# A retention layer and a squared-ReLU network on one core: filler matmuls from the first microseconds, another order of the loads, and a last output in three parts

## The chip, the core and the metric

The kernel runs on one core of one Trainium2 chip. The core has a matrix engine (PE, whose weight loads are listed as PEld), three engines for element-wise work (DVE, ACT, POOL), a queue engine (SP) that issues transfers, and 16 DMA engines that carry them between the main memory and the on-chip memory. Matrix products land in PSUM, of which the kernel holds four banks `fps` and two larger tiles, `sc` and `yy`. The metric is the device time of one execution in microseconds (us).

## The reference

Inputs are `q`, `k`, `v` of 4 x 8 x 768 x 64 floats (batch, head, time, width) and two weights of 512 x 2048 and 2048 x 512. The first half is a linear recurrence with a decay per head:

```python
for t in range(S):
    state = gamma[None, :, None, None] * state + np.einsum('bhd,bhe->bhde', k[:, :, t], v[:, :, t])
    y[:, :, t] = scale * np.einsum('bhd,bhde->bhe', q[:, :, t], state)
```

The second half takes the result with the heads side by side as `x` (3072 tokens x 512) and computes `h = max(x @ w_in, 0)` and `(h * h) @ w_out` in 32-bit floats.

## The kernel before, in words

**Tiling.** Time is cut into chunks of 128 tokens: 6 chunks for each of 4 batches, 24 in all (`m` or `n` below, 0 to 23). Within a chunk the recurrence becomes matrix products: scores of `k` against `q`, masked; values; and a state of 64 x 64 per head that is carried from chunk to chunk. Factors of the decay are multiplied in where `v` is cast (L434, L599) and where the result is read out (L573, L760). Matrices are cast from 32-bit to 16-bit floats on DVE, ACT or POOL (one helper, `copy_on`, L399 to L403), since PE works on 16-bit operands here.

The first four chunks go in pairs (0 with 1, 2 with 3): one load of 512 KB for each of `q`, `k`, `v` of a pair, transposes on PE (`T...`, L447), scores (`A`, L478), sums for the state (`B`, L494), values and the state's share (`C`, L504 and L515), read-out (`Y`). Later chunks have loads of 256 KB each (L588). Chunks 4 to 6 are transposed on PE through PSUM (L641), chunk 7 on PE as part of a visit (L614), and chunks 8 to 23 by a transposing DMA that SP issues (`X8` to `X23`, L632). A "visit" `V9.10` (L684, L695, L658, L673) finishes chunk 9 and does the scores of chunk 10; those need X10.

**The network.** Chunks are gathered in blocks (`BLOCKS`). `F1` (L807) is one group of the first product, 512 columns of PSUM: 8 matmuls of 256 columns in the first blocks, 4 of 512 or 16 of 128 in others. ACT applies the ReLU while it reads PSUM (L812), and DVE squares (L817). `F2.m.j` (L851) is a quarter of the second product of chunk `m`, 4 matmuls of 512 columns; its quarter `j` needs the weight slice `w_out j`. ACT copies the sum to an output tile `osb` (L859) and SP stores it (L863).

**Weights.** `w_in` comes in six pieces, four of 512 KB (`i0` to `i3`: the halves of its first two slices) and two of 1 MB (`i4`, `i5`); `w_out` in four of 1 MB (`o0` to `o3`). Each is cast in pieces (`cw...`) before use (L781 loads).

**Order.** All operations are put into a list with their dependencies, and `Plan.schedule` (L68) places them before the program is built, with assumed durations and an assumed model of the transfers. What comes out is a fixed order of instructions on each engine; each engine then runs its own in that order and waits for the data. `ORDER` (L228) fixes the order of the first loads on SP, all later transfers follow the plan, and `HOME` (L226) pins some casts to an engine. The same planner decides where "fillers" go: matmuls of the identity that nobody reads. The trace of before has two of them (L905), at 16.3 us.

```python
if WARM - WARMING < t < WARM + 1:
    o["fill"] = int(max(0.0, t - max(eng_free[eng], WARM - WARMING) - 0.1) / FILL)
```

Here `t` is the planned start of a PE operation, `WARM` is 20.0, `FILL` 0.215 and `WARMING` 5.5, so fillers stand between 14.5 and 21 us of the plan; they write to the last of four PSUM banks, which is kept free until then. The last chunk's output (`F2.23`) is made in two halves of 256 columns.

Of the kernel before, what the change touches and what calls it, by code (L numbers as in the profile page):

```python
# [14 lines left out]
AF = mybir.ActivationFunctionType  # L15
# [3 lines left out]
class Plan:  # L19
# [48 lines left out]
    def schedule(self, nbanks, max_open):  # L68
# [17 lines left out]
                    pool[e].add(o["i"])  # L86
        if "PE" in eng_free:
            eng_free["PE"] = 0.06 * PRE
        bank_free = [0.0] * (nbanks - 1) + [WARM + 1]
        bank_of = {}  # L90
        open_groups = set()
        closed = {}
# [5 lines left out]
        while done < n:  # L98
# [25 lines left out]
            if move:  # L124
# [4 lines left out]
                while sum(x[1] for x in out_) + n_desc > self.RING:  # L129
                    t = max(t, out_.pop(0)[0])  # L130
            start[i] = t
            b = o["bank"]
            if b is not None and b[0] == "open":
                k = min((x, j) for j, x in enumerate(bank_free) if x is not None)[1]
# [4 lines left out]
            if move:  # L139
                eng_free[eng] = t + hold  # L140
                if n_desc:
                    made = max(made, t + self.GEN_LATENCY) + gen
                    ready = made + 0.15
                else:
                    ready = t + hold + 0.5
                pipe = max(max(pipe, t + self.DMA_LATENCY) + cost, ready)
                late = [y for y in (max(max(y, t + self.DMA_LATENCY) + cost, ready) for y in late) if y > pipe + 0.05]
                end[i] = max([pipe] + late) + self.LAND
                out_.append((max([pipe] + late), n_desc))
                dur = hold  # L150
            else:
                if eng == "PE":
                    o["fill"] = 0
                    if WARM - WARMING < t < WARM + 1:
                        o["fill"] = int(max(0.0, t - max(eng_free[eng], WARM - WARMING) - 0.1) / FILL)
                    issued += 2 * o["fill"]
                    before = issued
                    todo, per = 2 * o["count"], dur / max(1, 2 * o["count"])
                    now = t
                    while issued + todo > edge:  # L160
                        step = max(0, edge - issued)
                        now = max(now + step * per, next_fetched)
                        issued, todo = max(issued, edge), todo - step
                        ahead = next((y for x, y in reversed(history) if x <= edge - self.AHEAD), 0.0)
                        ahead = max(ahead, crossed)
                        crossed = now
                        edge += self.BLOCK
                        next_fetched = ahead + min(5.7, max(0.3, pipe - ahead)) + self.FETCH
                    issued += todo
                    dur = now + todo * per - t  # L170
                    history.append((issued, t + dur))
                    if any(before < x <= issued for x in range(self.BLOCK0 - self.AHEAD, issued + 1, self.BLOCK)):
                        late.append(max(pipe, t + 0.4) + 1.27)
                    o["dur"] = dur
                eng_free[eng] = t + dur
                end[i] = t + dur + o["lat"]
# [26 lines left out]
AHEAD = 4  # L203
WARM = 20.0
FILL = 0.215
WARMING = 5.5
PACE = 8
LEAD = 2
NPE = 7
# [1 line left out]
PRE = 0  # L211
WHALF = 2
WHALFD = (0.60, 1.47, 33, 0.6)
CVT = {'DVE': 0.69, 'POOL': 1.1}
TCAST = {'DVE': 0.43, 'ACT': 0.63, 'POOL': 0.78}
TEVAC = {'ACT': 0.6, 'DVE': 0.62}
NPAIR = 2
F2LAG = 3.0
F2WAIT = 4
CAST = {"k": {"DVE": 0.43, "ACT": 0.63, "POOL": 0.78}, "q": {"DVE": 0.43, "ACT": 0.63, "POOL": 0.78}}  # L220
WCAST = {"DVE": 0.43, "ACT": 0.63, "POOL": 0.78}
EVAC = {"ACT": 0.6, "DVE": 0.62}
WPRIO = {"in": -2.0, "out": 2.0}


HOME = {'ck5': 'ACT', 'cq5': 'ACT', 'Eq0.0': 'DVE', 'cv0.0': 'DVE', 'ck0.0': 'DVE', 'cwin5.2': 'DVE', 'cv2.1': 'POOL', 'ck2.0': 'DVE', 'cwin5.0': 'DVE', 'cwin2.0': 'POOL', 'cwout0.3': 'POOL', 'cwin1.0': 'POOL', 'ck0.1': 'DVE', 'ck2.1': 'DVE'}  # L226
RANK = {}
ORDER = (  # L228
    "q0 k0 o0 i0 v0 q2 k2 o1 v2 i1 v4 i2 k4 i3 i4 q4 i5 k5 v5 v6 o2 o3 q5 v7 k6 q6 k7 q7"
)  # L230


# [8 lines left out]
def kernel(  # L241
# [279 lines left out]
    def pair_visits(m):  # L521
# [3 lines left out]
        for b2 in range(2):  # L525
            pl.add(f"A{m}.{b2}", "PE", 0.4, [f"qkT{q0}.{x}.{b2}" for x in "kq"] + [f"qkT{q0 + c}.{x}" for c in range(2) for x in "kq"],
                   banks[b2], lambda b2=b2: pair_scores(m, b2), prio=-300 + m, lat=0.25, count=16)
            for a in range(2):
                pl.add(f"P{m}.{b2}{a}", "DVE", 0.68, (banks[b2][a], "cmask2"), (f"ptp{w}.{b2}{a}",),
                       lambda b2=b2, a=a: nc.vector.tensor_tensor(  # L530
                           out=pts2[w][:, b2, a], in0=held_by[b2][:, a, :].rearrange("s (g j t) -> s g j t", g=2, j=2),
                           in1=cmask2[:, :, None, :].to_broadcast([P, 2, 2, C]), op=ALU.mult),
                       prio=urgency(m))
        tw = [f"twin{x}{w}.{b2}" for x in "kv" for b2 in range(2)]
        for c in range(2):
            if c == 1 and i + 1 == NCH - 1:
                continue
            o1 = {}
            i0 = pl.add(f"B{m + c}", "PE", 0.3, tw, (f"gB{m + c}",),
                        lambda c=c, o1=o1: pair_sums(m, c, fps[o1["op"]["bank_index"]]), prio=-290 + m, lat=0.25,  # L540
                        count=16, bank=("open", ("B", m + c), False))
            o1["op"] = pl.ops[i0]
            twin_users.append(i0)
            j0, j1 = state(m + c, 0), state(m + c + 1, 0)
            first = i + c == 0

            def add_up(j0=j0, j1=j1, first=first, o1=o1):
                cc = fps[o1["op"]["bank_index"]][:, 0:256].rearrange("s (p t) -> s p t", p=NJ)
                if first:
                    nc.vector.tensor_copy(sts[j1][:], cc)  # L550
                else:
                    nc.vector.tensor_tensor(out=sts[j1][:], in0=cc, in1=sts[j0][:], op=ALU.add)
            pl.add(f"S{m + c}", "DVE", 0.42, (f"gB{m + c}",) if first else (f"gB{m + c}", f"S{j0}"), (f"S{j1}",), add_up,
                   prio=urgency(m) - 0.5, bank=("close", ("B", m + c)))
        for b2 in range(2):
            def values_and_state(b2=b2):
# [272 lines left out]
    def rows(m):  # L829
        return where(m)[0] * S + where(m)[1] * C  # L830

    def ffn2(blk):
        for q4 in range(blk0[blk], blk0[blk] + blocks[blk]):
            g, u = divmod(q4, 4)
            h2 = h2s[g % NH2]
            slot = q4 % NOSB
            parts = 2 if q4 == NM - 1 else 1
            w = DM // parts
            for part in range(parts):
                ns = slice(part * w, part * w + w)  # L840
                grp = ("f2", q4, part)
                keys = [f"osb{slot}.{part}"] if parts > 1 else [f"osb{slot}.0", f"osb{slot}.1"]
                o1 = {}
                for j in range(4):
                    reads = [f"h{g % NH2}.{u}.{4 * j + c}" for c in range(4)] + [f"wout{j}.{c}.{h}" for c in range(4) for h in range(2)]

                    def mm(j=j, o1=o1, h2=h2, u=u, ns=ns, w=w):
                        ps = fps[o1["op"]["bank_index"]]
                        for c in range(4):
                            fb = 4 * j + c  # L850
                            nc.tensor.matmul(ps[:, 0:w], lhsT=h2[:, fb, u * C : u * C + C], rhs=w_out_bf[j][:, c, ns],  # L851
                                             start=(fb == 0), stop=(fb == NFB - 1))
                    i0 = pl.add(f"F2.{q4}.{j}" + f"/{part}" * (parts > 1), "PE", 0.866 / parts, reads, (f"g{grp}",), mm,
                                prio=(q4 + F2LAG) * 8 + 2 * j + 1 + part * 9, lat=0.2,
                                bank=("open", grp, True) if j == 0 else ("use", grp), count=4)
                    if j == 0:
                        o1["op"] = pl.ops[i0]
                pl.add(f"O{q4}" + f"/{part}" * (parts > 1), "ACT", 0.2 + 0.4 / parts, (f"g{grp}",), keys,
                       lambda o1=o1, slot=slot, ns=ns, w=w: nc.scalar.activation(  # L859
                           osbs[slot][:, ns], fps[o1["op"]["bank_index"]][:, 0:w], AF.Copy),  # L860
                       prio=q4, bank=("close", grp))
                pl.add(f"st{q4}" + f"/{part}" * (parts > 1), "SP", STORE, keys, (),
                       lambda q4=q4, slot=slot, ns=ns: nc.sync.dma_start(out[rows(q4) : rows(q4) + C, ns], osbs[slot][:, ns]),  # L863
                       prio=-1)

    dma_prio = {x: n for n, x in enumerate(dma_order(NM))}
# [30 lines left out]
    if tc is not None:  # L897
        with tc.manual_schedule():
# [3 lines left out]
            for i in sequence:  # L902
                o = pl.ops[i]
                for _ in range(o.get("fill", 0)):
                    nc.tensor.matmul(fps[NBANK - 1][:, 0 : 2 * P], lhsT=ident[:],  # L905
                                     rhs=ident[:, None, :].to_broadcast([P, 2, P]), start=True, stop=True)
                o["fn"](o["on"]) if o["flex"] else o["fn"]()
    return pl
# [30 lines left out]
```

## Time and profile before

| | |
|---|---|
| median of 11 runs | 214.1 us (213.31 to 215.58) |
| the profiled execution | 213.41 us, of which 211.6 us are the span from the first to the last instruction |
| busy in the span | PE 197.9 us (94%), DVE 115.9 (55%), ACT 88.1 (42%), POOL 40.1 (19%) |
| transfers | 38.13 MB, mean 180 GB/s |
| matmuls | 2570 |
| first matmul, last matmul's end | 5.62 us, 208.4 us |

Times in the profile count from the span's start. A PE that shows as busy is not at its peak by that: matmuls are pipelined and their ends are modelled, so the rate is read from the starts of groups that follow each other.

### The profile page before, as it was taken

The page shows a single profiled execution, that of the slowest core. Times are in us where ns is not written, and L with a number is a line of the kernel's source. Part 1 is how long each engine was busy: PE and PEld are TensorE (multiplying, and loading weights), DVE is VectorE, ACT ScalarE, POOL GpSimd, SP SyncE. Part 2 cuts the span into 40 slices and gives each one's busy share as a digit, 9 for nine tenths or more (in the row PEclk, how much of TensorE's full clock was granted, in tenths as well). Part 3 has the DMA queues.
Part 4 walks back from the last instruction along what each step waited for, and adds up shares of the span by engine and source line. Part 5 has one row for each costly group of instructions (what it writes and reads, how often), then busy time and mean ns, then how long its engine had stood idle before and what let it go on. Part 6 is the DMA issues. An engine that isn't in the chain of part 4 may idle for free.

```text
span 211.6 us, 5941 instructions
## 1 busy us (share of the span) xinstructions
PE 197.9 (94%) x2570; PEld 117.3 (55%) x2570; DVE 115.9 (55%) x253; ACT 88.1 (42%) x148; POOL 40.1 (19%) x69
## 2 busy tenths in 40 slices
PE   0679899998999999999999999999999999999993
PEld 0457686774676857676654444454444444444453
DVE  2686888746375977367670774746554432322100
ACT  8334485653342524434322455223534324534221
POOL 6345241124322130321220322021000000000000
PEclk9999999999999999999999999999999999999999
DMA  6999999999999999999999996999011011011022
GB/s 164 307 300 265 346 377 307 291 281 213 237 219 210 156 254 201 244 194 198 252 203 225 237 246 137 174 231 218 13 53 53 0 53 50 0 50 51 3 99 99
DMA packets 94442, 38.13 MB, mean 180 GB/s; under 512 B 79952, under 2 KB 88400, under 8 KB 94416
## 3 DMA queue, kind: packets, MB, share of 16 engines
q1 hardware_dynamic: 94416, 37.76, 81.2%
q8 instruction: 20, 0.33, 0.6%
q14 instruction: 6, 0.05, 0.1%
HBM read 27.26 MB, written 6.29 MB: 159 GB/s over the span
## 4 chain that ended last, share of the span: by engine, by line
PE 60%; SPq 22%; DMA 14%; issue 1%; POOL 1%; ACT 0%; POOLq 0%
PE fps L851 30%; PE fps L807 26%; SPq L588 11%; DMA qn<-in_q_dram 7%; DMA wst<-in_moe_w_out_dram 5%; SPq L781 4%; SPq L418 4%; DMA qkT<-kqs 3%; SPq L632 2%; PE yy L658 2%; SPq L863 1%; PE yy L673 1%; PE sc L684 1%; PE sc L695 1%; POOL w_out L403 0%
## 5 line engine op out<-in xcount | busy, mean ns | idle before, releaser
L807 PE MATMUL fps<-xt,w_in 128*128 128x256 bf16 (+2 forms) x640 | 93.6, 296 | 0.4 <-DVE xt L573 0.3
L851 PE MATMUL fps<-w_out,h 128*128 128x512 bf16 (+1 forms) x400 | 92.2, 371 | 0.7 <-POOL w_out L403 0.7
L812 ACT ACTIVATE h<-fps 128x512 bf16<-128x512 f32 x96 | 57.2, 596 | 76.7 <-PE fps L807 76.4
L807 PEld LDWEIGHTS <-w_in 128*128 128x128 bf16 x640 | 57.1, 98 | 31.1 <-issue 1.0
L817 DVE TENSOR_TENSOR h<-h 128x512 bf16<-128x512 bf16 x96 | 43.6, 462 | 50.4 <-ACT h L812 49.8
L851 PEld LDWEIGHTS <-h 128*128 128x128 bf16 x400 | 37.7, 98 | 37.4 <-issue 0.7
L859 ACT ACTIVATE osb<-fps 128x512 f32<-128x512 f32 (+1 forms) x25 | 14.5, 580 | 31.8 <-PE fps L851 31.5
L760 DVE TENSOR_TENSOR xt<-yy,yf 128x512 bf16<-128x512 f32 x20 | 13.7, 687 | 16.2 <-PE yy L673 12.0
L403 POOL CAST kqs<-kn 128x512 bf16<-128x512 f32 x19 | 12.0, 633 | 54.7 <-DMA kn<-in_k_dram 32.6
L403 POOL CAST kqs<-qn 128x512 bf16<-128x512 f32 x19 | 11.9, 628 | 20.5 <-DMA qn<-in_q_dram 20.5
L599 DVE TENSOR_TENSOR vs<-vn,vf 128x512 bf16<-128x512 f32 x20 | 13.6, 683 | 2.8 <-DMA vn<-in_v_dram 2.8
L751 DVE TENSOR_TENSOR state<-sc,state 128x256 bf16<-128x256 f32 x33 | 13.8, 418 | 0.5
L738 DVE TENSOR_TENSOR pt<-sc,cmask 128x512 bf16<-128x512 f32 x20 | 13.6, 680 | 0.0
L447 PE MATMUL fps<-ident,h 128*128 128x128 bf16 x32 | 4.6, 309 | 6.3 <-DVE h L401 6.3
L673 PE MATMUL yy<-qkT,state 64*64 64x64 bf16 x296 | 10.0, 197 | 0.2
L658 PEld LDWEIGHTS <-vs 64*64 64x64 bf16 x320 | 4.2, 107 | 6.9 <-issue 6.8
L399 ACT ACTIVATE qkT<-fps 128x512 bf16<-128x512 bf16 x8 | 4.7, 596 | 6.4 <-PE fps L447 4.9
L447 PEld LDWEIGHTS <-h 128*128 128x128 bf16 x32 | 3.0, 135 | 7.2 <-DVE h L401 6.5
L684 PE MATMUL sc<-qkT 64*64 64x64 bf16 x320 | 6.3, 194 | 0.4 <-DMA qkT<-kqs 0.4
L673 PEld LDWEIGHTS <-state 64*64 64x64 bf16 x296 | 6.2, 107 | 0.4 <-PE yy L673 0.4
L658 PE MATMUL yy<-pt,vs 64*64 64x64 bf16 x320 | 6.4, 198 | 0.0
L403 POOL CAST w_out<-wst 128x512 bf16<-128x512 f32 x5 | 3.7, 754 | 13.6 <-DMA wst<-in_moe_w_out_dram 13.6
(65 smaller groups left out, 87.0 us busy)
## 6 DMA issues: line engine op xcount, KB each, us to landing
out_dram<-osb SPq DMA_DIRECT2D x23, 256.0 KB, 3.7
vn<-in_v_dram SPq DMA_DIRECT2D x20, 256.0 KB, 4.9
kn<-in_k_dram SPq DMA_DIRECT2D x20, 256.0 KB, 4.8
qn<-in_q_dram SPq DMA_DIRECT2D x20, 256.0 KB, 5.2
wst<-in_moe_w_out_dram SPq DMA_DIRECT2D x4, 1024.0 KB, 9.7
wst<-in_moe_w_in_dram SPq DMA_DIRECT2D x4, 512.0 KB, 7.4
wst<-in_moe_w_in_dram SPq DMA_DIRECT2D x2, 1024.0 KB, 9.2
qn<-in_q_dram SPq DMA_DIRECT2D x2, 512.0 KB, 6.1
```

What stands on the lines that cost most here:

```text
L403: nc.gpsimd.tensor_copy(o, t)
L588: lambda x=x, t=t: nc.sync.dma_start(t.rearrange("s (h d) -> s h d", h=H), src[x][b, :, i * C : (i + 1) * C, :].rearrange("h s d -> s h d")),
L599: lambda: nc.vector.tensor_tensor(out=o[:], in0=t.rearrange("s (h d) -> s h d", h=H), in1=vf[:, i, :, None].to_broadcast([P, H, D]), op=AL ...
L658: nc.tensor.matmul(yy[L * c : L * c + L, sub, p * L : p * L + L], lhsT=vs[r, 4 * a + j, :], rhs=pt[r, a, j, :], start=(p == 0), stop=True, ...
L673: nc.tensor.matmul(yy[L * c : L * c + L, sub, p * L : p * L + L], lhsT=st[r, j, :], rhs=qkT[r, 1, j, sub * L : sub * L + L], start=False, ...
L751: f = lambda cc=cc, j1=j1, j0=j0: nc.vector.tensor_tensor(out=sts[j1][:], in0=cc, in1=sts[j0][:], op=ALU.add)
L760: lambda: nc.vector.tensor_tensor(out=xt[:, :, u * C : u * C + C].rearrange("s p (g t) -> s g p t", g=2), in0=yy[:, :, 0:256].rearrange("s ...
L807: nc.tensor.matmul(ps[:, u * n : u * n + n], lhsT=w_in_bf[j][:, cb, c * P : (c + 1) * P], rhs=xt[:, cb, cols], start=(cb == 0), stop=(cb = ...
L812: nc.scalar.activation(h2[:, f0 : f0 + per, cols], ps[:].rearrange("p (u n) -> p u n", u=per), AF.Relu)
L817: nc.vector.tensor_mul(hv, hv, hv)
L851: nc.tensor.matmul(ps[:, 0:w], lhsT=h2[:, fb, u * C : u * C + C], rhs=w_out_bf[j][:, c, ns], start=(fb == 0), stop=(fb == NFB - 1))
L859: lambda o1=o1, slot=slot, ns=ns, w=w: nc.scalar.activation(osbs[slot][:, ns], fps[o1["op"]["bank_index"]][:, 0:w], AF.Copy),
```

## The change

- Fillers may now stand from 1.6 us of the plan on (`WARMING` 18.4 in place of 5.5), that is, as soon as the identity is made, and in whichever PSUM bank is free. The program has 35 of them: 18 before the first transposes, 5 before the next two, then groups of 3, 1, 4, 2 and 2 up to `C2.0`.
- `ORDER`: `v0` goes ahead of the first half slice of `w_in`, which now lies between the loads of the two pairs; `k2` goes ahead of `q2`; `i2` and `i3` follow each other; `i5` goes ahead of `o0`, `q5` and `o2` ahead of `v5`; `v6` and `v7` move behind `o3`, `k6`, `q6` and behind `q7`.
- `HOME` keeps one pin; the planner chooses an engine for the other casts. One state copy may go to ACT. POOL's assumed time of a scaled cast is 1.3 in place of 1.1.
- The last chunk's output is made in three parts of 256, 128 and 128 columns, and the store of the last part is issued by ACT. PE has 2619 matmuls in all (2570 before): 35 fillers for 2, and 48 in the last chunk for 32.
- `ROUND` is an empty list, so the code under it is not used.

The planner makes its order anew with all this. Behind the first loads, SP's list differs by a few places: `X8` has one more load ahead of it (`v9`), `X9` the same transfers, `X10` one more store, `X11` one more store and one more load (`v12`). On PE, `V9.10` has 32 `F1` groups and 22 `F2` quarters ahead of it (32 and 21 before), `V10.11` 37 and 24 (34 and 23 before); at `F2.0.3`, `V5.6` and `V6.7` the counts are those of before.

```diff
-        bank_free = [0.0] * (nbanks - 1) + [WARM + 1]
+        bank_free = [0.0] * nbanks
...
                 if eng == "PE":
                     o["fill"] = 0
-                    if WARM - WARMING < t < WARM + 1:
+                    free = [(x, j) for j, x in enumerate(before_open) if x is not None and x <= max(eng_free[eng], WARM - WARMING)]
+                    if WARM - WARMING < t < WARM + 1 and free:
                         o["fill"] = int(max(0.0, t - max(eng_free[eng], WARM - WARMING) - 0.1) / FILL)
+                        o["fill_bank"] = min(free)[1]
...
-WARMING = 5.5
+WARMING = 18.4
...
-CVT = {'DVE': 0.69, 'POOL': 1.1}
+CVT = {'DVE': 0.69, 'POOL': 1.3}
...
+LAST = [256, 128, 128]
...
-HOME = {'ck5': 'ACT', 'cq5': 'ACT', 'Eq0.0': 'DVE', 'cv0.0': 'DVE', 'ck0.0': 'DVE', 'cwin5.2': 'DVE', 'cv2.1': 'POOL', 'ck2.0': 'DVE', 'cwin5.0': 'DVE', 'cwin2.0': 'POOL', 'cwout0.3': 'POOL', 'cwin1.0': 'POOL', 'ck0.1': 'DVE', 'ck2.1': 'DVE'}
+HOME = {'cwin0.2': 'DVE'}
+ROUND = []
 RANK = {}
 ORDER = (
-    "q0 k0 o0 i0 v0 q2 k2 o1 v2 i1 v4 i2 k4 i3 i4 q4 i5 k5 v5 v6 o2 o3 q5 v7 k6 q6 k7 q7"
+    "q0 k0 v0 i0 k2 q2 v2 i1 i2 i3 k4 v4 i4 q4 i5 o0 k5 o1 q5 o2 v5 o3 k6 q6 v6 k7 q7 v7"
 )
...
-            parts = 2 if q4 == NM - 1 else 1
-            w = DM // parts
-            for part in range(parts):
-                ns = slice(part * w, part * w + w)
+            widths = LAST if q4 == NM - 1 else [DM]
+            parts = len(widths)
+            for part, w in enumerate(widths):
+                lo = sum(widths[:part])
+                ns = slice(lo, lo + w)
...
-                pl.add(f"st{q4}" + f"/{part}" * (parts > 1), "SP", STORE, keys, (),
-                       lambda q4=q4, slot=slot, ns=ns: nc.sync.dma_start(out[rows(q4) : rows(q4) + C, ns], osbs[slot][:, ns]),
+                at_end = parts > 1 and part == parts - 1
+                pl.add(f"st{q4}" + f"/{part}" * (parts > 1), "ACT" if at_end else "SP", STORE, keys, (),
+                       lambda q4=q4, slot=slot, ns=ns, at_end=at_end: (nc.scalar if at_end else nc.sync).dma_start(
+                           out[rows(q4) : rows(q4) + C, ns], osbs[slot][:, ns]),
                        prio=-1)
...
-                    nc.tensor.matmul(fps[NBANK - 1][:, 0 : 2 * P], lhsT=ident[:],
+                    nc.tensor.matmul(fps[o["fill_bank"]][:, 0 : 2 * P], lhsT=ident[:],
                                      rhs=ident[:, None, :].to_broadcast([P, 2, P]), start=True, stop=True)
```

## The prediction

> **What bounds the kernel now.** I read the page's slices first, then PE in order of time, PE's waits, the chain that ended last, and the issues of single transfers.
>
> ```profile
> PE   0679899998999999999999999999999999999993
> PEclk9999999999999999999999999999999999999999
> DMA  6999999999999999999999996999011011011022
> ```
>
> PE is full from the fifth slice (21 us) to the last. The transfers are full in the first 24 slices (127 us). So this is no kernel with idle engines in its middle: it has a start of some 20 us, a stretch in which full transfers and a full PE run against each other, and a long stretch of PE alone. The clock row says 9 from the first slice on; the rows of PE in time say otherwise:
>
> ```profile
> 17.87 1.89 PE L807 MATMUL fps<-xt,w_in 128*128 128x256 bf16 x8
> 19.68 0.54 PE L478 MATMUL yy<-qkT 64*64 64x128 bf16 x16
> 20.06 0.57 PE L494 MATMUL fps<-h 64*64 64x64 bf16 x32
> 20.56 1.05 PE L807 MATMUL fps<-xt,w_in 128*128 128x256 bf16 x8
> ```
>
> The same eight matmuls take 1.81 us from start to the next start at 17.87 and 0.87 later (24 of them start at 36.12, the next group at 38.74). PE runs at half rate until about 19.7 us. Between 5.0 and 19.7 us it is listed busy for 11.19 of 14.70 us.
>
> What does PE wait for after that? Its list of waits has these from the main part:
>
> ```profile
> PE fps L851 <- POOL w_out L403: 0.7, 1, 0.7
> ...
> PE sc L684 <- DMA qkT<-kqs: 0.4, 2, 0.2
> PE fps L807 <- DVE xt L573: 0.3, 1, 0.3
> ```
>
> The first is `F2.0.3`, waiting for the last slice of `w_out`, the second the scores of chunks 9 and 11, waiting for X9 and X11. The issues of three single transfers (line, size, us to landing) and PE's row show the first:
>
> ```profile
> wst<-in_moe_w_out_dram SPq DMA_DIRECT2D x1, 1024.0 KB, 8.3
> ...
> qn<-in_q_dram SPq DMA_DIRECT2D x1, 256.0 KB, 6.2
> ...
> wst<-in_moe_w_out_dram SPq DMA_DIRECT2D x1, 1024.0 KB, 9.5
> ...
> 48.11 1.89 PE L851 MATMUL fps<-w_out,h 128*128 128x512 bf16 x8 [0.71 <-POOL w_out L403]
> ```
>
> `o2` was issued at 33.80 and landed at 42.1, `q5` at 36.96 and 43.2, `o3` at 37.64 and 47.1. They land one behind the other, whatever the time of issue: 256 KB took 1.05 us there, 1 MB 2.8 (`o2`, 39.3 to 42.1) and, for `o3`, 3.95. In the window of `o3` the transfers list one 16 KB packet of the instruction queue (20 of them in all); I take the 1.15 us of excess for its doing, not proved. The chain shows the second:
>
> ```profile
> 66.83 7.42 DMA qn<-in_q_dram
> 74.26 0.03 issue
> 74.28 0.02 POOLq L403
> 74.30 0.08 issue
> 74.38 0.62 POOL kqs L403
> 75.02 6.05 DMA qkT<-kqs
> 81.12 0.32 PE sc L684 x16
> ```
>
> From 81.12 on PE waits for nothing more, and its last matmul ends at 208.41: 127.29 us of work. So the end is set by when PE gets through 48.11 and 81.12, and both were set by landings. PE's slow start is 28 us ahead of the first.
>
> **The change, part by part.** The sum is against the profiled execution: span 211.6, time 213.41, which is 0.69 under the median of 214.1.
>
> *Fillers.* Two fillers at half rate took 16.30 to 16.73, 0.215 each. Eighteen from 1.66 (POOL has made the identity) last to 5.53, and the first transposes wait for a DVE cast until 5.62: nothing on the path, 0.1 at worst. The 17 others fill gaps (6.7 to 7.4, 9.8 to 11.0 and on); five at half rate take 1.08 us in a gap of 0.66, so up to 0.4 late once. If PE comes to full rate by 8 us in place of 19.7, then by 25 us it gains: `F1.0.0` 1.81 to 0.87 (0.94), and on the path from `C0.0` to `A2.0` four times four transposes 0.47 to 0.23 and two `C` from 1.05 to 0.73 (1.6, of which the casts between them leave perhaps two thirds). About 2.0 us. But who is next? PE is free for `F2.0.3` at 47.40 and waits to 48.11. Arriving 2.0 earlier it waits 2.7. So I take 0 for the fillers; the other end is the full 2.0.
>
> The Trainium skill ("TensorE: Matmul & The Clock Gate", Part 1) says that PE starts at half its clock, comes to full after some 3.4 us of sustained work and falls back after as long an idle window. The rows at 17.87 and 20.56 agree with two rates. By the rule alone, as an estimate, the gate opens 3.4 us or a little more after the fillers begin, and the sum would be lower by those 2 us; the row of 48.11 takes them back.
>
> *Loads.* The first pair's `v` lands third, at 8.4 (as `i0` does now) and not at 10.2, and `i0` at 10.2. `F1.0.0`, its user, comes at 15 to 18, so no loss. `i5` and `o0` change places (1 MB each); `F2.0.0` has 15 `F1` groups ahead in place of 12, so it can wait. What counts is how much lies ahead of `o3`: six loads of 512 KB, six pieces of `w_in` (4 MB), three of `w_out` (3 MB) and seven loads of 256 KB were 11.75 MB. Now six of 256 KB: 11.5 MB, as `v6` and `v7` have moved behind. `o3` lands 1.05 us earlier, at 46.1, `F2.0.3` starts at 47.06, with the same work behind it. `q7`, which `V5.6` needs (its cast ended at 53.43, the visit began at 54.08), has one load less ahead of it too (`v7`), so it keeps its distance. Gain 1.05. The bounds: if the 1.15 of excess falls elsewhere, 2.2; if it falls twice ahead of `o3`, -0.1 (a loss).
>
> *X9 to X11.* X9 has the same transfers ahead, and PE three more `F2` quarters before it needs it (2.6 us): the wait of 0.20 is gone. X10 has one more store ahead (0.65 us, the distance of landings 56.55 to 57.20): 75.16 becomes 75.8, and PE comes at 76.52 - 1.05 - 0.20 + 0.87 = 76.14. X11 has a store and a 256 KB load more (0.65 + 1.2): 81.07 becomes 82.9. PE has three `F1` and one `F2` more ahead of it, 4 x 0.867 = 3.47: it comes at 80.94 - 1.25 + 3.47 = 83.16. So both land just in time, with 0.3 us to spare, and the two waits of 0.4 together go. Gain 0.40; the bounds are 0.40 and, with 1.15 of excess on X11, -0.5.
>
> *Casts and engines.* `HOME`, `CVT` and the state copy on ACT move work of 0.4 to 1.5 us between engines that are idle half of the time, ahead of 47 us; the wait at `F2.0.3` hides up to 0.71 of it, plus what the fillers bring. Without that cover a POOL cast (0.62) in place of a DVE one (0.42) costs 0.2 each time it lies on the path. I take 0.
>
> *Last output.* 16 matmuls of 256 columns took 1.73 us; 32 of 128 take 1.78, by the rate of L807 with 128 columns (16 from 45.97, less its end: 0.89). +0.05.
>
> ```profile
> 208.41 0.38 ACT L859 ACTIVATE osb<-fps 128x256 f32<-128x256 f32 x1 [1.31 <-PE fps L851]
> ...
> out_dram<-osb SPq DMA_DIRECT2D x1, 128.0 KB, 1.7
> ```
>
> The last eviction shrinks from 0.38 to about 0.27 (512 columns took 0.60, so 0.22 per 256). A 256 KB store on idle engines took 2.0 and 128 KB 1.7, so 64 KB perhaps 1.55. Together -0.26. SP issued 0.02 after the eviction, so ACT saves at most that; what a first transfer of ACT costs no row shows. The nearest: the first load of SP took 4.4 us to land, the shortest in a full stretch 3.55, so up to 0.9 more. I take 0, being nearer to SP's stores at the end, which go out in 0.34 each.
>
> The Trainium skill speaks against that edit ("DMA: Bandwidth & Descriptors", Issuing engines are not separate DMA queues): transfers of all issuers run on the same engines, and another issuer saves only the time of issue. SP has nothing else to do there (its longest waits are those for ACT's `osb`), so by the rule the edit brings nothing.
>
> Sum: -1.05 - 0.40 + 0.05 - 0.26 = -1.66 us. The profiled execution would be 211.75, the median 212.4.
>
> **The rivals.**
>
> *B: PE's start counts.* If landings were earlier than I reckon (the excess gone, 2.2 in place of 1.05), the fillers' gain is used: PE would reach `F2.0.3` at 45.4, and 2.7 of the 2.8 us up to there could be had. With the last output's 0.2 and the waits' 0.1 to 0.4: -3.0, 211.1. For it: the excess is not inherent. Against: the transfers are full to 127 us and a faster PE moves no byte.
>
> *C: the excess moves.* One more 1.15 ahead of `o3` or on X11 eats most: PE has 98 more instructions (49 matmuls and their weight loads), some of them early. -1.66 + 1.15 = -0.5: 213.6.
>
> *D: X11 late, slower.* From 83.2 on, each microsecond of X11 is one of the end: 127.29 - 3.47 + 0.05 of work lie behind. SP's longest hold for a cast ahead of an X is 2.1 us. If one more of these (2.1) and one excess (1.15) come ahead of X11, it lands at 86.15 and the last matmul ends at 210.0, 1.6 later than now; with the last output -0.3, 215.4. It decides from 85.7 on (slower by over 0.5%). For it: X11's place on SP is two transfers later, and its reserve is 0.3.
>
> *E: the fillers do not hold the rate up.* Then PE is up to 2.0 later at 25 us, but it is before `F2.0.3` that it waited: by my forecast no change of the time. This tells A from B.
>
> **How the numbers follow.** A (forecast, -1.0 to -2.3, with E in it) 0.52; B 0.18; C 0.17; D 0.13. Half a per cent, 1.07 us, is about what a measurement of this kernel can tell from no change. A lies beyond that for all but 0.04, B wholly: faster 0.66. C and the rest of A: same 0.20. D with some of C: slower 0.14. A's own range is 211.8 to 213.1. For 8 in 10: the low end is B with 0.3 for the medians' scatter, 210.8; the high end takes in C and half of D, 214.7.
>
> **What would show it.** In the profile after: rows of L807 x8 at 0.87 a group from the first one on; `o3` landing at about 46 and PE's `F2.0.3` near 47, with a wait of 1 us or more ahead of it although PE is faster in the start; no wait of over 0.3 for X9 to X11, X11 landing near 83; 124 us of work behind it. If `F2.0.3` starts without a wait, B is right. If PE waits for X11 by over 1 us, D is. If the rows up to 20 us stay at half rate and the time falls all the same, E is, and the fillers are idle weight.

## The result and the profile after

The kernel after takes 211.13 us (median of 12 runs, 210.64 to 211.39) against 213.88 us (47 runs, 212.71 to 215.58): ratio 0.9863, 95% interval 0.9842 to 0.9883, or 2.75 us less. The forecast was 212.4. The profiled execution took 210.96 us with a span of 209.2 (before: 213.41 and 211.6), so there the difference is 2.4 to 2.45; the rest of the 2.75 is where the two profiled executions lie in their own scatter.

Source lines have moved: L822 is `F1` (was L807), L867 `F2` (L851), L656 the transposes of chunks 4 to 6 (L641), L699 the scores (L684), L875 and L880 the last eviction and its store (L859, L863), L408 a cast on POOL (L403), L923 a filler.

The slices of the page (5.2 us each): PE has 6 to 8 tenths to 37 us with one 9 between, and 9 from there to the last slice; the transfers are full for nearly 28 slices, 146 us (before, too, they are full up to the 28th, with one slice of 6 tenths between).

```profile
PE   6787898999999999999999999999999999999994
...
DMA  6999999999999999999998999999711011011022
```

PE in order of time (start, duration): 18 fillers, the transposes behind them, the next five fillers, and the first group of `F1`.

```profile
1.72 4.02 PE L923 MATMUL fps<-ident 128*128 128x256 bf16 x18 [1.72 <-POOL ident L339]
5.53 1.06 PE L452 MATMUL fps<-ident,h 128*128 128x128 bf16 x8
6.38 0.84 PE L923 MATMUL fps<-ident 128*128 128x256 bf16 x5
...
14.81 1.04 PE L822 MATMUL fps<-xt,w_in 128*128 128x256 bf16 x8
```

From start to start, the 18 fillers take 0.21 each and the eight transposes 0.107; of the five fillers at 6.38 the first takes 0.21, the second 0.14, the others 0.11, and the transposes at 7.71 stand 0.056 apart. So in this execution PE is at full rate from about 6.65 us on, 4.9 us after the first filler; `F1.0.0` has it too (1.04 listed, 1.89 before) and starts at 14.81 in place of 17.87. So far the fillers do what they should. PE's list of waits from 12 to 50 us shows where that lead went (total, times, longest):

```profile
PE fps L822 <- POOL w_in L408: 1.2, 3, 0.5
PE fps L499 <- POOL h L439: 0.7, 1, 0.7
PE fps L656 <- POOL kqs L408: 0.5, 1, 0.5
PE fps L452 <- ACT h L404: 0.4, 1, 0.4
PE fps L452 <- POOL h L408: 0.2, 1, 0.2
```

Three waits of `F1` for casts of `w_in` and one of the transposes of `k5`. In order of time the four rows with a wait behind 19 us are these; the landings ahead of them are those of `i1` (18.39), `i3` (21.67), `i4` (26.47) and `k5` (34.94):

```profile
19.11 1.05 PE L822 MATMUL fps<-xt,w_in 128*128 128x256 bf16 x8 [0.36 <-POOL w_in L408]
...
22.40 1.92 PE L822 MATMUL fps<-xt,w_in 128*128 128x256 bf16 x16 [0.53 <-POOL w_in L408]
...
27.45 1.05 PE L822 MATMUL fps<-xt,w_in 128*128 128x256 bf16 x8 [0.29 <-POOL w_in L408]
...
35.89 0.40 PE L656 MATMUL fps<-ident,kqs 128*128 128x128 bf16 x4 [0.49 <-POOL kqs L408]
```

The wait for `w_out` is not in the list any more: `F2.0.3` (second row) follows `F1` with none, and the transposes of `k6` follow 0.2 later than PE alone would have it.

```profile
45.79 1.00 PE L822 MATMUL fps<-xt,w_in 128*128 128x128 bf16 x15
46.63 1.03 PE L867 MATMUL fps<-w_out,h 128*128 128x512 bf16 x4
47.71 0.40 PE L656 MATMUL fps<-ident,kqs 128*128 128x128 bf16 x4
```

The chain that ended last comes through the landing of `k6` and its cast; from there on it is work of PE and of what feeds it:

```profile
37.92 8.81 DMA kn<-in_k_dram
46.73 0.05 issue
46.78 0.88 POOL kqs L408
47.66 0.04 issue
47.71 0.40 PE fps L656 x4
```

The issues of the two single transfers that land there, `o3` and `k6` (size, us to landing):

```profile
wst<-in_moe_w_out_dram SPq DMA_DIRECT2D x1, 1024.0 KB, 10.1
...
kn<-in_k_dram SPq DMA_DIRECT2D x1, 256.0 KB, 8.8
```

`o3` was issued at 35.53 and landed at 45.58, `k6` at 37.92 and 46.73. `o3` lands 2.80 after the transfer ahead of it (3.95 before) and is cast by 46.5: `o3`, `k6` and PE come to 46.6 us within a few tenths of each other.

Around the scores of chunk 11, the same chain runs through PE alone; before, it came through X11:

```profile
76.10 1.83 PE fps L867 x8
77.93 4.37 PE fps L822 x40
82.30 0.25 PE yy L673 x16
82.55 0.06 PE yy L688 x8
82.61 0.13 PE sc L699 x16
```

The chain counts a piece from the end of the one before it; by their own row the scores start at 82.44:

```profile
82.44 0.30 PE L699 MATMUL sc<-qkT 64*64 64x64 bf16 x16
```

X11 lands at 81.64, 0.80 ahead of that. The end of the program, in order of time:

```profile
206.28 0.28 ACT L875 ACTIVATE osb<-fps 128x128 f32<-128x128 f32 x1 [0.62 <-PE fps L867]
206.58 0.38 ACTq L880 DMA_DIRECT2D out_dram<-osb  x1
```

### The profile page after: what moved, and what is told of

Its sections match the earlier page's. It is cut to its first block, busy times and chain, and to the rows that moved or that the text cites. A ratio compares the mean times of both kernels' runs of the same rounds, so it can differ in the third digit from the quotient of the medians.

```text
span 209.2 us, 6038 instructions
## 1 busy us (share of the span) xinstructions
PE 199.8 (96%) x2619; PEld 118.4 (57%) x2619; DVE 116.0 (55%) x252; ACT 87.8 (42%) x148; POOL 43.3 (21%) x71
## 4 chain that ended last, share of the span: by engine, by line
PE 75%; DMA 17%; SPq 4%; POOL 1%; ACT 1%; issue 0%; DVE 0%; ACTq 0%
PE fps L867 37%; PE fps L822 32%; DMA kn<-in_k_dram 14%; DMA qn<-in_q_dram 4%; PE yy L673 2%; SPq L796 2%; SPq L423 2%; PE yy L688 1%; PE sc L710 1%; POOL kqs L408 1%; PE sc L699 1%; ACT qkT L635 0%; DVE xt L775 0%; PE fps L656 0%; PE yy L629 0%
## 5 line engine op out<-in xcount | busy, mean ns | idle before, releaser
L822 PE MATMUL fps<-xt,w_in 128*128 128x256 bf16 (+2 forms) x640 | 92.5, 294 | 1.3 <-POOL w_in L408 1.2
L867 PE MATMUL fps<-w_out,h 128*128 128x512 bf16 (+2 forms) x416 | 91.8, 363 | 0.0
L822 PEld LDWEIGHTS <-w_in 128*128 128x128 bf16 x640 | 56.6, 98 | 31.4 <-POOL w_in L408 1.9
L867 PEld LDWEIGHTS <-h 128*128 128x128 bf16 x416 | 37.9, 98 | 37.2 <-issue 0.3
L875 ACT ACTIVATE osb<-fps 128x512 f32<-128x512 f32 (+2 forms) x26 | 14.7, 565 | 35.9 <-PE fps L867 35.9
L408 POOL CAST kqs<-kn 128x512 bf16<-128x512 f32 x20 | 13.4, 670 | 50.5 <-DMA kn<-in_k_dram 46.8
L408 POOL CAST kqs<-qn 128x512 bf16<-128x512 f32 x20 | 13.4, 671 | 29.0 <-DMA qn<-in_q_dram 29.0
L923 PE MATMUL fps<-ident 128*128 128x256 bf16 x35 | 7.0, 352 | 1.7 <-POOL ident L339 1.7
L710 PE MATMUL sc<-vs,kqs 64*64 64x64 bf16 x288 | 6.2, 193 | 0.0
L699 PE MATMUL sc<-qkT 64*64 64x64 bf16 x320 | 6.2, 193 | 0.0
L406 DVE CAST w_out<-wst 128x512 bf16<-128x512 f32 x8 | 4.7, 632 | 2.6 <-DMA wst<-in_moe_w_out_dram 2.4
L408 POOL CAST w_in<-wst 128x512 bf16<-128x512 f32 x6 | 4.2, 698 | 8.5 <-DMA wst<-in_moe_w_in_dram 8.5
```

The source lines that it names most:

```text
L408: nc.gpsimd.tensor_copy(o, t)
L822: nc.tensor.matmul(ps[:, u * n : u * n + n], lhsT=w_in_bf[j][:, cb, c * P : (c + 1) * P], rhs=xt[:, cb, cols], start=(cb == 0), stop=(cb = ...
L875: lambda o1=o1, slot=slot, ns=ns, w=w: nc.scalar.activation(osbs[slot][:, ns], fps[o1["op"]["bank_index"]][:, 0:w], AF.Copy),
```

## The experiments

Two theories stood after the result. **A**: landings, one behind the other, set when PE gets through 47 us; the fillers buy nothing. **B**: the landings came early enough that PE's faster start counts. B's number, 211.1, was what the clock showed, so the number alone could not decide.

### Are the fillers used?

**`e1_no_fill`**: the kernel after, its plan untouched, without the 35 fillers.

```diff
-                for _ in range(o.get("fill", 0)):
+                for _ in range(0):
```

> The changed kernel with the 35 fillers left out; order of every other instruction and transfer as planned. Theory A (the load stream sets when PE gets through 46 to 48 us, the fillers buy nothing): PE runs at half rate up to some 15 to 19 us, its rows up to 25 us are 1 to 2 us later, the waits for w_in3 (0.53), w_in4 (0.29) and k6 (0.5) shrink by that, Tk6 starts within 0.3 us of 47.7, and the median is 211.0 to 211.6. Rival B (PE's start counts now that o3 is no longer late): Tk6 and all behind it 1 to 2 us later, median 212.2 to 213.2. What would be left of the gain of 2.75 us without the fillers is 2.2 or more by A and 0.7 to 1.6 by B.

Measured: 210.87 us (210.59 to 210.98), ratio 0.9881 [0.9847, 0.9914]. `F1.0.0` and `F1.0.2` in order of time, then PE's waits from 12 to 50 us:

```profile
15.56 1.92 PE L822 MATMUL fps<-xt,w_in 128*128 128x256 bf16 x8
...
20.26 0.94 PE L822 MATMUL fps<-xt,w_in 128*128 128x256 bf16 x7
```

```profile
PE fps L656 <- POOL kqs L408: 0.4, 1, 0.4
PE sc L509 <- DVE h L545: 0.3, 1, 0.3
PE yy L509 <- DVE h L545: 0.2, 1, 0.2
```

PE is at half rate to about 19 us and 1.15 us late at `F1.0.2`; it then waits 0.9 us in all (0.39 of it for `q5`, at 39.56) where the kernel after waits 3.0. `F2.0.3` starts at 46.60 (after: 46.63) and everything behind it lies within 0.04 us. A holds, B falls.

**`e2_before_fill`**: the kernel before, its plan untouched, with fillers put into the gaps that the plan has on PE (35 in all).

```diff
+    pe_end = 1.6
+    for i in sequence:
+        o = pl.ops[i]
+        if o["on"] == "PE":
+            if pl.start[i] < 20.5:
+                o["fill"] = max(o["fill"], int(max(0.0, pl.start[i] - pe_end - 0.1) / FILL))
+            pe_end = pl.start[i] + o["dur"]
```

> The kernel before with 35 fillers put into PE's planned gaps up to 20 us (18, 5, 2, 6, 2, 2), its order of instructions and transfers unchanged. Theory A: F1.0.0 and what follows up to 25 us come 1.5 to 2.5 us earlier, F2.0.3 then waits for o3 for 2 us or more in place of 0.7 and starts where it did (48.1 give or take 0.6, with the excess on o3), median 213.2 to 214.2 (no change). Rival B: the gain is passed on, median 211.8 to 212.8.

Measured: 212.94 us, ratio 0.9983 [0.9953, 1.0012], no change that can be told. The median lies between the two forecasts; the interval leaves at most 1.0 us of gain, where B asked for 1.1 to 2.1. `F1.0.0` starts 1.7 earlier (16.16), `V.4` 1.1 (31.05), `F2.0.3` 0.54 (47.57), `V5.6` 0.31 (53.77): the lead melts from landing to landing. The 0.54 at `F2.0.3` is not PE's lead: `o3` itself landed 0.55 earlier in this execution (46.59), and its cast ended when `F2.0.3` began. Its 18 first fillers are the same as those of the kernel after, but they take less time:

```profile
1.71 3.41 PE L912 MATMUL fps<-ident 128*128 128x256 bf16 x18 [1.71 <-POOL ident L334]
```

Here the full rate comes at 4.4 us, 2.7 us after the first filler, and not 4.9 as in the kernel after.

### Is it the landings?

**`e10_one_more_load`**: a load of 256 KB more ahead of `o3`.

```diff
+                if o["name"] == "ldwout3":
+                    nc.sync.dma_start(osbs[2][:].rearrange("s (h d) -> s h d", h=H), q[1, :, 0:C, :].rearrange("h s d -> s h d"))
```

> The kernel after, with one load of 256 KB more on SP's queue just ahead of the last slice of w_out (o3); it writes a buffer that nothing reads before its first output. Theory A (the end is set by how many bytes land ahead of o3, k6 and what follows): o3 lands 1.05 to 1.2 us later (46.7), k6 the same (47.8), F2.0.3 starts near 47.6, the transposes of k6 near 48.8, X9 to X11 each about 1.1 later; the time rises by 0.7 to 1.2 us, to 211.6 to 212.3. Theory B (PE's own pace up to 47 us sets the end, landings only follow): the time stays within 0.3 us of the kernel after.

Measured: 213.05 us, ratio 0.9938 [0.9912, 0.9963]; against the after's 0.9863 that is 0.75% or 1.6 us more (1.9 by the medians). `o3` lands at 47.08 (+1.50), `F2.0.3` starts at 48.05, `V6.7` at 59.53 (+2.12). A's sign, but more than A said. Of the 1.50, about 1.1 goes with the load (0.68 of its own, 0.40 more for `o3` behind it) and 0.4 with a later landing of `o2`. The rest comes behind: SP issued `v6` 1.9 us later (to 47.02, after: 45.13), the landing of `v6` was 2.38 behind the one ahead (after: 1.43), `q7` landed at 54.10 (51.46), and the chain goes through it:

```profile
48.07 6.03 DMA qn<-in_q_dram
54.10 0.05 issue
54.16 0.63 POOL kqs L408
54.78 0.04 issue
54.83 0.32 PE yy L629 x16
```

**`e12_skip_k4_v4`** and **`e13_skip_no_fill`**: the other way, 512 KB less ahead of the fifth slice of `w_in`, with and without fillers. `after_again` is the kernel after on the same chip.

```diff
+                if o["name"] in ("ldk4", "ldv4"):
+                    continue
```

> The kernel after without the loads of k4 and v4 (512 KB, 1.94 us of landings ahead of the fifth slice of w_in); chunk 4 is computed from old contents of its buffers, so that part of the output is left wrong and only the time counts. Theory A (landings bind up to 47 us, fillers' gain is spent waiting): all landings from the fifth slice of w_in on come 1.9 earlier, the waits for it (0.46), for k5 (0.67) and for k6 (0.2 to 0.5) go, F2.0.3 starts at 45.3 to 45.6 as PE's own pace then binds, and the time falls by 1.0 to 1.5 us. Theory B (PE's pace already sets F2.0.3): F2.0.3 stays near 46.6, the time within 0.3.

> The same without the loads of k4 and v4 (chunk 4 computed from old contents) and without the fillers. Theory A: with the landings out of the way the fillers' gain should show, so this one is 0.5 to 0.8 us slower than the same kernel with fillers, F2.0.3 near 46.0, the time 0.3 to 0.8 below the kernel after. The rival (the fillers' gain is lost for another reason than landings, for instance because PE's rows after 20 us are slower): both kernels without the two loads take the same time within 0.2.

> The kernel after, unchanged, on the chip of the three others of this set, for direct comparison: 210.9 to 211.3 us by every theory, F2.0.3 near 46.6.

Measured: with fillers 209.16 us (208.84 to 209.54), without 209.88 (209.67 to 209.99), `after_again` 211.14 (210.93 to 211.86). `F2.0.3` with fillers:

```profile
44.58 1.03 PE L867 MATMUL fps<-w_out,h 128*128 128x512 bf16 x4
```

and without:

```profile
45.75 1.03 PE L867 MATMUL fps<-w_out,h 128*128 128x512 bf16 x4
```

With the landings out of the way PE waits from 22 to 50 us for 0.2 in the first and nothing in the second; PE's own pace sets 47 us, and the fillers are worth 0.72 us of the time by the medians (1.17 at `F2.0.3` in the two traces, which are the shortest execution with fillers and the longest without). Both fell by more than I had written (2.0 and 1.3 for 1.0 to 1.5 and 0.3 to 0.8), the difference between them came as written. So the fillers work; in the kernel after their gain is spent waiting.

### What of the other edits?

**`e3_before_order`**: the kernel before with the new `ORDER` alone, planned anew. (`ORDER` ranks the loads, and the planner may issue one later than its place in it: in the trace of before `o0` comes behind `q4` and `o1` behind `k5`.)

```diff
-    "q0 k0 o0 i0 v0 q2 k2 o1 v2 i1 v4 i2 k4 i3 i4 q4 i5 k5 v5 v6 o2 o3 q5 v7 k6 q6 k7 q7"
+    "q0 k0 v0 i0 k2 q2 v2 i1 i2 i3 k4 v4 i4 q4 i5 o0 k5 o1 q5 o2 v5 o3 k6 q6 v6 k7 q7 v7"
```

> The kernel before with ORDER of the changed one and nothing else (two fillers, its pins, two halves at the end); the planner makes its order anew. Theory A: o3 lands near 45.6 to 46.1, F2.0.3 at 46.6 to 47.3 although PE is at half rate up to about 19 us, no wait of over 0.3 for X9 to X11; median 211.6 to 212.8, that is 1.1 to 2.3 of the 2.75 us. Rival B (both are needed: order and rate): median 213 to 214, under 0.9 of it.

Measured: 211.94 us, ratio 0.9933 [0.9912, 0.9955], that is 1.4 of the 2.75 us. `V5.6` starts at 52.55, as in the kernel after (52.58), but with 11 `F2` quarters ahead of it where the kernels before and after have 12: of the 1.5 us gained by there, 0.87 is work put off. At `V17.18`, where the same work lies behind, it is 1.9 us later than the kernel after (130.98, after: 129.11): that quarter, and 1.08 us at `F1.6.0` (92.45), which is a new line in PE's waits from 58 us on:

```profile
PE fps L807 <- DVE xt L760: 0.9, 1, 0.9
```

The chain behind it goes through the landing of a `v` at 91.10. X11 lands at 84.14, but the scores that need it start at 84.96 and wait for nothing. This traced execution took 213.07 us, 1.1 over the median of its ten; the nine others took 211.69 to 212.11, so the wait may be its own. By the medians the order alone lacks 0.8 us of the whole change, some 0.3 of it the last output's.

**`e4_after_old_order`**: the opposite, the kernel after with the old `ORDER` (the diff of `e3` the other way round).

> The changed kernel with ORDER of before (42 fillers by the planner's count); the planner makes its order anew. Theory A: o3 lands at 46.5 to 48, F2.0.3 at 47.5 to 49 after a wait of 1 us or more, and the time is that of before or worse: 213.5 to 216. Rival B: the fillers' gain remains, 211.8 to 212.8.

Measured: 216.17 us, ratio 1.0114 [1.0066, 1.0162]. `o3` lands at 48.16, `F2.0.3` starts at 50.18, and PE's waits have

```profile
PE sc L699 <- DMA qkT<-kqs: 1.8, 2, 1.0
...
PE fps L656 <- POOL kqs L408: 1.6, 2, 1.4
```

That is worse than the forecast. The traced execution is the longest of four (215.08 to 217.27), and PE fell back to half rate in it, behind two waits: 16 matmuls of 128 columns took 1.55 us to the next start at 46.35 and 0.89 at 51.05, and the granted clock is 0.57 from 46 to 50 us.

```profile
46.12 0.40 PE L656 MATMUL fps<-ident,kqs 128*128 128x128 bf16 x4 [1.44 <-POOL kqs L408]
46.35 1.76 PE L822 MATMUL fps<-xt,w_in 128*128 128x128 bf16 x16
```

How much of the loss is owed to that is not shown, since `o3` landed late as well.

About half of the gain comes with the order of the loads alone, and none is left without it. Its worth depends on the plan around it: 1.4 us with the old pins and fillers, 5 us with the new ones.

**`e8_after_old_pins`**: the kernel after with the old pins, the old cost of a POOL cast and the state copy on DVE.

```diff
-CVT = {'DVE': 0.69, 'POOL': 1.3}
+CVT = {'DVE': 0.69, 'POOL': 1.1}
-HOME = {'cwin0.2': 'DVE'}
+HOME = {'ck5': 'ACT', 'cq5': 'ACT', 'Eq0.0': 'DVE', 'cv0.0': 'DVE', 'ck0.0': 'DVE', 'cwin5.2': 'DVE', 'cv2.1': 'POOL', 'ck2.0': 'DVE', 'cwin5.0': 'DVE', 'cwin2.0': 'POOL', 'cwout0.3': 'POOL', 'cwin1.0': 'POOL', 'ck0.1': 'DVE', 'ck2.1': 'DVE'}
-            pl.add(f"S{m + c}", {"DVE": 0.42, "ACT": 0.45} if first else "DVE", 0.42, ...
+            pl.add(f"S{m + c}", "DVE", 0.42, ...
```

> The kernel after with the pins (HOME), the cost of a POOL cast (CVT) and the state copy of the kernel before; loads, fillers and last output are those of after, and the plan is made anew. The forecast put these three edits at 0: the time within 0.3 us of the kernel after, X11 landing near 82 as the queue of SP is the same up to it. The rival (the 1 us that the load order alone lacked against the kernel after, behind 75 us, comes of these edits): X11 lands 2 us later, V10.11 starts near 84.5, and the time is 1.0 us above the kernel after.

Measured: 211.39 us, ratio 0.9860 [0.9822, 0.9899], that of the kernel after (0.9863); the median is 0.26 higher, within the 0.3 of the forecast. X11 lands at 81.89. The three edits are worth little beside the new order. What `e3` lacks is therefore not owed to the pins. Its plan was made without the new fillers and the new last output; `e1` shows that the fillers on the chip are not it either. Which of the planner's choices it was I have not separated.

**`e5_after_two_parts`**: the last output in two parts, both sent by SP. **`e6_after_sp_store`**: three parts, the last sent by SP.

```diff
-LAST = [256, 128, 128]
+LAST = [256, 256]
```

```diff
-                at_end = parts > 1 and part == parts - 1
+                at_end = False
```

(The first has both diffs.)

> The kernel after with the last output in two parts of 256 columns as before, both sent by SP. By the forecast's terms for the last output (+0.05 for more matmuls, -0.11 for the shorter eviction, -0.15 for the smaller store, 0 for the issuer) the last matmul ends 0.05 earlier and the end comes 0.2 to 0.3 us later than in the kernel after. The rival (the first transfer of ACT has a cost that eats the gain, as the bound of 0.9 allowed): no change or faster.

> The kernel after, the last 64 KB sent by SP and not by ACT. By the forecast the issuer is worth 0 (at most 0.02 for SP, up to 0.9 for ACT's first transfer): the time within 0.15 us of the kernel after, the last landing 1.5 to 1.7 us from its issue. The rival (ACT's issue saves a hand-over, as the edit means it to): 0.2 us slower or more.

Measured, on the same chip: 211.53 us (211.21 to 212.53) with two parts, 210.96 (210.93 to 211.79) with three sent by SP; the kernel after has 211.13. From the start of the last eviction to the end of the span: two parts 206.25 to 209.4, 3.2; three with SP 207.15 to 210.0, 2.9; three with ACT 206.28 to 209.2, 2.9. The parts are worth 0.3, the issuer nothing. (The profiled execution of `e6` is the longest of its six. What makes it late lies ahead of the last output, where its program is the kernel after's: it is 0.26 us later at `V5.6`, and at the scores of chunk 11 PE waits 0.43 for X11, which lands at 83.27; from there on it is 0.87 us later.) The transfers after 206 us in `e6`, by SP:

```profile
out_dram<-osb SPq DMA_DIRECT2D x2, 64.0 KB, 1.6
```

and in the kernel after, by ACT:

```profile
out_dram<-osb ACTq DMA_DIRECT2D x1, 64.0 KB, 1.6
```

### A version from the findings

**`e11_no_fill_k6_dve`**: `e1` with the cast that the chain of after runs through, that of `k6`, moved from POOL (0.87) to DVE.

```diff
+    for o in pl.ops:
+        if o["name"] == "ck6":
+            o["on"] = "DVE"
```

> A version pointed to by the runs: the kernel after without fillers, and with the cast of k6 on DVE, where it takes 0.42 us, in place of POOL, where it took 0.87. By theory A the wait of 0.4 to 0.5 ahead of Tk6 goes, of which PE's own end of F2.0.3 leaves 0.2 to be had: 0.0 to 0.25 us below the kernel after. The rival (DVE's square of chunk group 2, which runs from 46.75 to 47.18, is ahead of it or is pushed behind it): 0.0 to 0.3 slower.

Measured: 211.16 us (210.93 to 211.38), beside `after_again` at 211.14 on the same chip. No gain. I had misread the wait: the 0.4 to 0.5 in the list are not those of `k6` but of `k5` or `q5`. In order of time, the rows with a wait between 34 and 50 us are these two, chunk 5's, and `V5.6` starts at 52.70 (52.73 in `after_again`):

```profile
35.93 0.40 PE L656 MATMUL fps<-ident,kqs 128*128 128x128 bf16 x4 [0.54 <-POOL kqs L408]
40.14 0.40 PE L656 MATMUL fps<-ident,kqs 128*128 128x128 bf16 x4 [0.32 <-POOL kqs L408]
```

Apart from the two that leave loads out, no version beats the kernel after by more than the scatter; `e1`, with 35 matmuls less, is its equal.

## Why the prediction was right, and where its steps were off

The sum of the prediction against the same stretches of the two profiled executions (starts of PE's operations; us):

| step | forecast | measured |
|---|---|---|
| fillers and loads, to `F2.0.3` | -1.05 | 48.11 to 46.63: -1.48 |
| `F2.0.3` to `V6.7` | 0 | 10.74 to 10.78: +0.04 |
| X9 to X11, `V6.7` to `V17.18` | -0.40 | 72.41 to 71.70: -0.71 |
| `V17.18` to the last quarter of the last output's first part | 0 | 74.75 both: 0 |
| from there to the last eviction | +0.05 | 2.39 to 2.43: +0.04 |
| last eviction to the end | -0.26 | 3.2 to 2.9: -0.27 |
| sum | -1.66 | -2.38 (spans: -2.4) |

**Direction and mechanism** hold: the order of the loads carries the gain (`e3` has half of it by the order alone, `e4` none without it), it acts by what lands ahead of the loads that PE needs up to 47 us (`e10`, `e12`), the fillers bring nothing as long as landings bind (`e1`, `e2`), the pins little (`e8`), the issuer of the last store nothing (`e6`).

**The number was in part luck.** 211.13 lies outside the 211.8 to 213.1 that I gave A, and inside the whole range only because that range was drawn to take in B, which is wrong. B's number does not even follow from its own condition: `o3` landing 2.2 earlier puts `F2.0.3` at 45.9, a gain of 2.2 and not of 2.7, and the sum at 211.3 to 211.6. (D's limit is off, too: by its terms, 127.29 - 3.47 + 0.05 of work and 0.26 gained at the end, X11 would decide from 85.9 on and not from 85.7; nothing rests on that.)

**The first term was mis-sized**, -1.05 for -1.48. I counted the load that moved away and left the excess of 1.15 on `o3` where it was. `o3` landed 1.55 earlier: 1.02 for the load, 1.15 for the excess gone from it (its gap 3.95 to 2.80), less 0.87 of excess back at `o0` (2.71 to 3.58); the last 0.25 is what is left of shifts among the others (`i1` took 1.46 more, `i2` 1.32 and `i4` 0.59 less). No run moved `v6` alone, so the load's share is read from the traces. The prediction had this as a bound (2.2) and as half of rival B. And an earlier `o3` alone would not have done: PE was free for `F2.0.3` at 47.40 before, so it had to come 0.8 earlier itself. That too came with the order. I had costed the earlier `v0` (8.51 for 10.20) at nothing, "no loss"; but `C0.0`, which needs it, starts at 11.44 in `e1`, without fillers, and at 10.62 in `e3`, with the two of before, against 13.25 before, and at 13.21 in `e4` with fillers and the old order. By 30 us (`V.4`) the order alone has PE at 30.65, the whole change at 30.61, before had 32.16.

**The doubt on that excess is now smaller.** I had put it down, unproved, to a 16 KB packet of the instruction queue. Two pairs of kernels have the same queue of loads and differ only in fillers, which shift the packets (each is listed with 0.9 to 1.6 us in the kernel after). After and `e1`: the packet at 29.08 moves to 32.61, and the late landing moves from `o0` (3.58, then 2.83) to `o1` (2.81, then 3.58). Before and `e2`: the packet at 44.16 is gone from there (37.73 and 48.54 in `e2`), the gap of `o3` falls from 3.95 to 2.78, and `k7`, which landed 1.13 behind its forerunner, now lands 2.04 behind. So late landings go with the packets, by 0.75 to 1.15 us some 2 to 5 us later. Which load is late is not fixed by that: with the packet at 28.96 and 29.32, `e10` and `e6` have `i5` late (31.21 and 31.51), not `o0`; with it at 32.58, `e11` has `k5` late (35.21), not `o1`. Not each packet has a late landing (that of 34.23 in before and of 38.32 in after have none), and no run changed the packets alone.

**The second term was mis-sized** too, -0.40 for -0.71. I took the listed waits (0.2 each). By starts of groups that follow each other, the two visits of before with a wait took 1.03 and 0.99 (`V8.9`, `V10.11`), the two without 0.67 (`V7.8`, `V9.10`): a wait of 0.2 cost PE 0.3 to 0.4. That X10 and X11 would come "just in time" held, X11 with 0.80 to spare and not 0.3: X11 landed at 81.64 for 82.9, since there was less excess ahead of it than in the trace of before.

**My test for B was a wrong one.** "If `F2.0.3` starts without a wait, B is right": it started without a wait, the time was B's 211.1, and B is wrong all the same. The step that failed is "arriving 2.0 earlier it waits 2.7": I let PE's lead travel untouched from 25 to 47 us and be lost in one place. It was lost before, in the waits ahead of 19.1, 22.4, 27.5 and 35.9 us for slices of `w_in` and for `k5`; by starts the last three cost 0.71, 0.46 and 0.67. So the landings that hold PE in the kernel after are `i3`, `i4` and `k5`, and `o3` and `k6` come just in time behind them; `e12` takes bytes away ahead of `i4`, and all these waits shrink together. Rival E's sentence was the better test: the start slow, the time the same. It was right of the time (`e1`), though not of its condition, since the fillers do hold the rate.

C's price (excess moving to X11) and D (X11 late) did not come in the traced execution of the kernel after; that of `e6`, the same program up to the last output, shows that their place is real: X11 lands 1.6 later there (83.27) and PE waits for it.

**Clock and issuers.** The nine traced executions that begin with the 18 fillers come to full rate 2.7 to 5.6 us after the first one, 4.9 in the kernel after. The Trainium skill ("TensorE: Matmul & The Clock Gate", Part 1) has full clock after some 3.4 us of sustained work; that lies within this spread, but four executions were clearly earlier (2.7 to 3.2, in `e2`, `e8`, `e10` and `e12`). By the estimate from the rule alone the fillers would have brought 2 us; `e1` measures none, `e13` against `e12` 0.72 with loads taken away. The 64 KB of the last store land in 1.6 us from SP (`e6`) and from ACT (the kernel after). That agrees with the Trainium skill ("DMA: Bandwidth & Descriptors", Issuing engines are not separate DMA queues), by which all issuers' transfers run on the same engines.

## What to carry to other kernels

Before you pay for a faster engine, take away its inputs' lateness in an experiment (drop a load that lies ahead) and see whether the faster engine then shows; if it doesn't, the transfers bind, and a lead is spent a few tenths at a time in every wait on the way. Where transfers land one behind the other, count the bytes ahead of each needed one: here one load of 256 KB moved behind them let `o3` land 1.0 us earlier. PE had 0.7 us of slack ahead of it, so PE had to come earlier as well, and earlier landings in the start saw to that. And test a mechanism by taking it out of the changed kernel, not by the number it would give: here a wrong rival had the right time.

## What the runs showed of the hardware

- A packet of the instruction queue (16 KB, 20 in a run) goes with a later landing of a data transfer, 0.75 to 1.15 us, though not each packet and not always the same load. 35 fillers (70 PE instructions with their weight loads) move a packet from some 33 us to 29, and the late landing with it: 35.2 to 38.1 us in three traces without the early fillers (`e1`, `e3`, `e11`), 31.2 to 33.8 in three of the kernel after's start with them (the kernel after, `e6`, `e10`). The Trainium skill ("Runtime: NRT & Kernel Launch", Instruction fetch mechanics) has the refill in 16 KiB blocks of 256 instructions and calls the cost of crossing a block mostly hidden. PE shows no stop for it: in the kernel after its list of waits is empty from 52 us on, with 15 of the packets there. The transfers do.
- The same 18 fillers from 1.7 us on bring PE to full rate between 4.4 us (`e2`) and 7.3 us (`e6`), by the execution. No run explains the spread.
- With fillers in the start the granted clock falls back in some executions. It is listed with 0.982 to 0.992 in 21 of 64 of the kernels that begin with them, and with 0.997 or more in all 71 of those that don't (26 of `e1`, `e3`, `e11` and `e13`, 45 of the kernel before). As an estimate, 0.992 of 210 us is what 3.4 us at half rate give; `e4`'s trace shows such a stretch from 46.5 us on. In `e12` the three so listed took 209.27 to 209.54 us and the three others 208.84 to 209.04; in the kernel after no cost is seen (210.93, 211.14 and 211.22 among 210.64 to 211.39). Why it falls back is not shown.
- The listed wait of an engine understates its cost: 0.2 us of wait on a transposing DMA cost PE 0.3 to 0.4 us, and the three of 0.53, 0.29 and 0.49 in the kernel after cost 0.71, 0.46 and 0.67.
- The first transfer that ACT issues in the program (64 KB, at 206.58) lands as fast as one of SP, 1.6 us; I had left up to 0.9 open for it.
- The kernel after's runs scatter over 0.75 us (12 runs), those of before over 2.9 us (47 runs). `e6`'s trace shows 0.8 us of such scatter made by landings, 0.6 of it by X11 alone; for the kernel before no run explains it.
